# Windowed attention and a gated feed-forward layer on one core: a new order and new engines for every step, and the seven-product form from the fifth chunk on

## The chip, the core and the metric

One core of a Trainium2 chip runs the whole program. The metric is the device time of one execution in microseconds; less is better. The median of three runs of the kernel before is 890.99 us (888.37 to 891.76). The engines are TensorE (PE, with its weight loads as PEld), VectorE (DVE), ScalarE (ACT), GpSimd (POOL) and SyncE (SP), which here only issues DMAs.

## The reference

```
scores = q @ k^T / 8                        # 8 x 8 heads, 576 positions, 64 dims
scores = where(0 <= i - j < 64, scores, -1e9)
attn   = softmax(scores);  x = attn @ v     # x: 4608 tokens x 512
h   = x @ w_in                              # 512 -> 2048
g   = h * erf(softplus(h))
out = g @ w_out                             # 2048 -> 512
```

The inputs q, k and v are 32-bit floats, w_in and w_out 64-bit floats.

## The kernel before

All products on PE are made from 16-bit halves: each operand is scaled by a power of two and split into a high half and a low half, and three products (high by high, high by low, low by high) are summed. The other engines mostly make these halves.

**Weights.** Sixteen pieces of w_in and w_out are fetched by SP (L519), turned from 64-bit to 32-bit floats by DVE and ACT (L523, L527, L531), bounded (L537), and split: a high half (L346 on ACT, L348 on DVE, L350 on POOL) and a low half (L353 on DVE, or by PE at L580 and L581 and an eviction). PE fills the waits of this stage with warm-up products (L747).

**Attention**, in 36 tiles of 128 tokens. SP loads q, k and v; ACT or DVE take their largest magnitudes (L371, L373); a short chain of small DVE and PE steps (L380 to L398) makes the scales of a chunk of 256 tokens; q, k and v are split into halves (high: L346, L348 or L350; low: L353, always DVE). PE makes the scores (L425), DVE adds the mask and takes the maxima (L434), DVE or POOL subtracts them (L439), ACT takes the exponential (L443), and the result is split (L472, L474 or L476, and the remainder at L450 on DVE or POOL), turned by a DMA (L453) and multiplied with v (L460). DVE normalizes (L465 to L468); x is split (L472 or L474, L495) and turned by a DMA (L499).

**Feed-forward**, in 36 groups g: 18 chunks c of 256 tokens, each with the two halves of the 2048 hidden columns. The first matmul exists in two forms. The plain form (`mm1`, L620) has 4 pieces of 24 matmuls of 256 columns, and each piece is evicted once by ACT or DVE (`hidden`, L472 or L474). The seven-product form (`product`, L673) has 7 products of 24 matmuls of 128 columns; its inputs are sums of blocks of x (`x_sums`, L482) and of w_in (`w_sums`, L654 and L658, 72 steps in all, made once and kept in the three buffers named stage), and its outputs are 4 evictions (`take`, L472 or L474) and 3 additions on DVE (`add`, L689). Then come softplus and erf on ACT (L698, L702), the gate product on DVE (`gate`, L707), a high half (`g_hi`) and a low half (`g_lo`) of the gate, the second matmul with 16 + 8 matmuls of 512 columns in each half (`mm2`, L730), and the result on ACT or DVE (L346, L348, L739). ACT has to load another table when it goes from one of softplus, erf and exponential to another (ACT_TABLE_LOAD).

The constant `FAST` says from which chunk on the seven-product form is used; the chunks before it use the plain form. It also decides how the gate is split. In the plain chunks the high half is a scaling and the low half is always a SCALAR_TENSOR_TENSOR of DVE (L353); in the others the high half is a plain narrowing on ACT, DVE or POOL (L472, L474, L476), and the low half is a subtraction on DVE or POOL (L721):

```
def g_lo(g, n, eng="v"):
    if ORDER[g][0] < FAST:
        rest(glb[:, sl], yat(g, n), st_s[g][:, n:n + 1], ghb[:, sl])
    else:
        eng_of(eng).tensor_tensor(glb[:, sl], yat(g, n), ghb[:, sl], op=ALU.subtract)
```

**Order.** The string `PLAN` is the program: a list of steps such as `gl:14:0:g` (low half of the gate, group 14, half 0, on GpSimd; v is DVE, a is ACT) or `S:0:4:v` (step 4 of the sums of quarter 0 of w_in, on DVE). A loop at the end issues them one after the other, so the order of steps in the string is the order in every engine's queue and in the DMA queue of SP. Nothing is reordered later, and each engine works its queue in order. The short names that are used below: `mm` and `mw` are the pieces of the first matmul in its plain and its seven-product form, `mA` and `mB` the second matmul with the high and with the low half of the gate, `gh` and `gl` those halves, `xw` the additions at L689, `S` the sums of w_in, `xd` those of x, `dc` and `gn` small scale factors (L603, L609, L610), `h` the high halves of the weights, and `px` the small reduction at L388 and L389 inside the chain that makes a chunk's scales.

Of the kernel before, what the change touches and what calls it, by code (L numbers as in the profile page):

```python
# [18 lines left out]
B, H, S, D = 8, 8, 576, 64  # L19
W = 64  # L20
# [24 lines left out]
FAST = 5  # L45
# [770 lines left out]
```

## Time and profile before

| | |
|---|---|
| median of three runs | 890.99 us |
| the profiled execution, its own time | 889.82 us |
| its span, first to last instruction | 888.0 us |
| granted TensorE clock, mean | 0.988 |
| ACT table loads | 116 |
| matmuls in the first matmul, plain and seven-product | 960 and 4368 |

A row of a group gives the line, the engine, the operation, out<-in, shapes and count, then the busy time in us and the mean of one in ns, then the idle time of the engine just before them with what ended it. A row of the timeline gives the start and the length in us. A row by stage gives the start and end of the stage and its length, and then, for each engine, its busy time with the number of instructions in brackets.

### The profile page before, as it was taken

The page shows a single profiled execution, that of the slowest core. Times are in us where ns is not written, and L with a number is a line of the kernel's source. Part 1 is how long each engine was busy: PE and PEld are TensorE (multiplying, and loading weights), DVE is VectorE, ACT ScalarE, POOL GpSimd, SP SyncE. Part 2 cuts the span into 40 slices and gives each one's busy share as a digit, 9 for nine tenths or more (in the row PEclk, how much of TensorE's full clock was granted, in tenths as well). Part 3 has the DMA queues.
Part 4 walks back from the last instruction along what each step waited for, and adds up shares of the span by engine and source line. Part 5 has one row for each costly group of instructions (what it writes and reads, how often), then busy time and mean ns, then how long its engine had stood idle before and what let it go on. Part 6 is the DMA issues. An engine that isn't in the chain of part 4 may idle for free.

```text
span 888.0 us, 25679 instructions
## 1 busy us (share of the span) xinstructions
PE 845.5 (95%) x10915; PEld 594.2 (67%) x10915; DVE 760.8 (86%) x1623; ACT 656.9 (74%) x810; POOL 348.4 (39%) x276
## 2 busy tenths in 40 slices
PE   7879888999999999999899999999999999999998
PEld 4557566556666686766676776767776776777673
DVE  5999998999988999999888989897999898874642
ACT  6989987999796979787777876686656674673452
POOL 0315132621252246652336623075947262541201
PEclk9899999999999999999999999999999999999999
DMA  9985783343431646554536745445545452412000
GB/s 361 299 215 148 222 164 111 72 121 83 132 73 35 150 109 126 133 103 108 114 97 138 160 122 120 103 85 138 115 108 114 108 104 59 90 39 55 1 25 24
DMA packets 160515, 103.97 MB, mean 117 GB/s; under 512 B 137744, under 2 KB 137872, under 8 KB 160400
## 3 DMA queue, kind: packets, MB, share of 16 engines
q1 hardware_dynamic: 160400, 102.33, 47.0%
q8 instruction: 85, 1.39, 0.7%
q14 instruction: 30, 0.25, 0.1%
HBM read 59.44 MB, written 9.44 MB: 78 GB/s over the span
## 4 chain that ended last, share of the span: by engine, by line
PE 49%; DVE 25%; ACT 13%; DMA 5%; issue 5%; POOL 4%; SPq 0%; DVEq 0%; POOLq 0%; ACTq 0%
PE o L730 23%; PE hp L673 16%; PE hp L620 5%; ACT y L698 3%; DVE y L707 2%; DVE sm L434 2%; ACT L698 2%; DVE vs L353 2%; DVE h L689 2%; DVE p L450 2%; PE av L460 1%; ACT y L702 1%; PE s L425 1%; ACT L702 1%; DMA w<-w_in 1%
## 5 line engine op out<-in xcount | busy, mean ns | idle before, releaser
L730 PE MATMUL o<-w,gh 128*128 128x512 f16 x1152 | 260.7, 379 | 2.1 <-ACT gh L346 1.6
L730 PEld LDWEIGHTS <-gh 128*128 128x128 f16 x1152 | 109.7, 98 | 124.3 <-ACT gh L346 1.7
L673 PEld LDWEIGHTS <-w 128*128 128x128 f16 x2496 | 146.4, 98 | 22.8 <-issue 8.9
L673 PE MATMUL hp<-xt,w 128*128 128x128 f16 x2496 | 154.8, 220 | 6.4 <-DVE h L689 4.0
L730 PE MATMUL o<-w,gl 128*128 128x512 f16 x576 | 136.2, 379 | 0.0
L620 PE MATMUL hp<-xt,w 128*128 128x256 f16 x960 | 113.1, 277 | 6.7 <-ACT ks L346 3.7
L673 PE MATMUL hp<-xt,stage 128*128 128x128 f16 x1872 | 113.8, 219 | 4.1 <-DMA xt<-xs 2.4
L673 PEld LDWEIGHTS <-stage 128*128 128x128 f16 x1872 | 108.0, 98 | 13.1 <-issue 5.8
L721 POOL TENSOR_TENSOR gl<-y,gh 128x1024 f16<-128x1024 f32 x36 | 82.0, 2283 | 71.9 <-DVE gh L474 34.3
L620 PEld LDWEIGHTS <-w 128*128 128x128 f16 x960 | 94.0, 99 | 24.3 <-issue 7.7
L439 POOL TENSOR_TENSOR sm<-sm,mx 128x512 f32<-128x512 f32 x44 | 53.6, 1227 | 109.8 <-DVE mx L434 98.9
L698 ACT ACTIVATE y<-h,c 128x1024 f32<-128x1024 f32 x72 | 79.9, 1143 | 22.5 <-DVE h L474 22.1
L472 ACT ACTIVATE h<-hp 128x512 f32<-128x512 f32 x99 | 57.9, 587 | 51.6 <-PE hp L673 45.0
L730 PEld LDWEIGHTS <-gl 128*128 128x128 f16 x576 | 53.3, 98 | 54.3
L707 DVE SCALAR_TENSOR_TENSOR y<-h,cy,y 128x1024 f32<-128x1024 f32 x52 | 70.7, 1378 | 20.2 <-ACT y L702 19.8
L443 ACT ACTIVATE sm<-sm,shift,cde 128x512 f32<-128x512 f32 x72 | 57.4, 809 | 26.7 <-DVE sm L439 13.6
L702 ACT ACTIVATE y<-y 128x1024 f32<-128x1024 f32 x72 | 74.0, 1051 | 0.5
L689 DVE TENSOR_TENSOR h<-hp,h 128x512 f32<-128x512 f32 x78 | 53.1, 683 | 20.0 <-PE hp L673 13.1
L434 DVE CUSTOM_DVE_ANT_0 sm<-s,mask 128x128 f32<-128x128 f32 x288 | 65.1, 285 | 4.8 <-PE s L425 4.3
L698 ACT ACT_TABLE_LOAD x43 | 55.2, 1283 | 13.6 <-DVE h L474 8.5
L476 POOL TENSOR_SCALAR gh<-y 128x1024 f16<-128x1024 f32 x14 | 19.6, 1401 | 97.9 <-DVE y L707 97.9
L702 ACT ACT_TABLE_LOAD x44 | 56.5, 1283 | 0.8
(153 smaller groups left out, 1372.5 us busy)
## 6 DMA issues: line engine op xcount, KB each, us to landing
vr<-v_in SPq DMA_DIRECT2D x36, 512.0 KB, 4.3
kr<-k_in SPq DMA_DIRECT2D x36, 384.0 KB, 3.7
qr<-q_in SPq DMA_DIRECT2D x36, 256.0 KB, 3.4
out<-ob SPq DMA_DIRECT2D x36, 256.0 KB, 2.4
stage<-w_out SPq DMA_DIRECT2D x6, 1024.0 KB, 6.1
stage<-w_in SPq DMA_DIRECT2D x5, 1024.0 KB, 10.1
w<-w_in SPq DMA_DIRECT2D x2, 1024.0 KB, 11.5
w<-w_out SPq DMA_DIRECT2D x2, 1024.0 KB, 5.9
```

Of the source, the lines that this page charges most:

```text
L434: nc.vector.tensor_tensor_reduce(smi(u, par)[:, j, :], sps[par][:, j, :], mask[:, var, :], 1.0, LOWEST, op0=ALU.add, op1=ALU.max, accum_ou ...
L439: eng_of(eng).tensor_tensor(s, s, m.unsqueeze(2).broadcast_to([P, HP, P]), op=ALU.subtract)
L443: nc.scalar.activation(s, s, AF.Exp, bias=shift14, scale=es)
L472: nc.scalar.activation(dst, src, AF.Copy)
L620: nc.tensor.matmul(hps[pc % 2][:, f, :], w1[a][:, cc, fs], xt[b][c % 2][:, cc:cc + 5:4, :], start=(n == 0), stop=(n == 3 * NCC - 1))
L673: nc.tensor.matmul(dst, w, xt[b][c % 2][:, blk + cc, :], start=bool(first) and at + cc + a + b == 0, stop=at + cc + a == 3 * P + 2, skip_g ...
L689: nc.vector.tensor_tensor(dst, bank_of((1, 0, 1)[i]), dst, op=ALU.add)
L698: nc.scalar.activation(yat(g, n), at(hb, g, n), AF.Softplus, scale=st_c[g][:, n:n + 1])
L702: nc.scalar.activation(y, y, AF.Erf)
L707: nc.vector.scalar_tensor_tensor(y, at(hb, g, n), s, y, op0=ALU.mult, op1=ALU.mult)
L721: eng_of(eng).tensor_tensor(glb[:, sl], yat(g, n), ghb[:, sl], op=ALU.subtract)
L730: nc.tensor.matmul(ops[j], a[:, f, ts], w2[b][:, hf * GF + f, :], start=f == 0 and a is gh and b == 0, stop=f == GF - 1 and a is gl)
```

## The change

The whole of `PLAN` is written anew, and `FAST` goes from 5 to 4. No function is edited; since the string is one line longer, a line L of the kernel before is line L+1 in the changed kernel.

```
-FAST = 5
+FAST = 4
...
-    "gh:2:0:v mA:1:1 t:6:1 gl:1:1 er:2:1 gl:2:0 S:0:4:v sp:3:0 gt:2:1 a:6:0 sp:3:1 a:6:1 mB:1:1 pk:9:0:v gh:2:1:g "
...
+    "mA:35:0 gh:35:1:a mB:35:0 gl:35:1:v mA:35:1 mB:35:1 fo:35:0:v fo:35:1:v st:17:0 st:17:1 "
```

With `FAST` at 4, chunk 4 (groups 8 and 9) takes the seven-product form: 8 plain pieces go and 14 products come, with 6 additions, and the x of chunk 4 needs block sums. The sums of w_in must then be ready two groups earlier. Counted over the whole string, the steps move between engines as follows (before, after):

| step | ACT | DVE | POOL |
|---|---|---|---|
| low half of the gate (`gl`) | 0, 0 | 36, 50 | 36, 22 |
| high half of the gate (`gh`) | 43, 50 | 12, 11 | 17, 11 |
| sums of w_in (`S`) | 10, 8 | 35, 41 | 27, 23 |
| split of q, k, v, high half | 66, 73 | 28, 18 | 14, 17 |
| exponential, narrowing (`ec`) | 37, 28 | 18, 18 | 17, 26 |
| exponential, remainder (`r`) | 0, 0 | 40, 36 | 32, 36 |
| evictions of the first matmul (`ev`, `ew`) | 99, 97 | 45, 47 | 0, 0 |
| additions of the first matmul (`xw`) | 0, 0 | 78, 84 | 0, 0 |
| high half of the weights (`h`) | 10, 9 | 1, 5 | 5, 2 |
| largest magnitudes (`pk`) | 51, 57 | 57, 51 | 0, 0 |
| small scale factors (`dc`) | 0, 0 | 25, 15 | 11, 21 |

The built program holds 129 table loads on ACT, against 116, and 301 warm-up matmuls, against 293.

The first place is POOL's queue at groups 14 and 15. Before:

```order
L495 TENSOR_TENSOR xs_0_130<-x,xs_0_128 128x512
L721 TENSOR_TENSOR gl<-y_143,gh 128x1024
L721 TENSOR_TENSOR gl<-y_144,gh 128x1024
L439 TENSOR_TENSOR sm_118<-sm_118,mx_92 128x512
L450 TENSOR_TENSOR p_1_122<-sm_118,p_1_120 128x512
L482 TENSOR_TENSOR x<-x 128x256
L721 TENSOR_TENSOR gl<-y_142,gh 128x1024
L350 TENSOR_SCALAR ks_0_108<-kr_100,csc 128x768
L610 TENSOR_SCALAR sg<-kwo,cde,wm_67 128x1
L721 TENSOR_TENSOR gl<-y_143,gh 128x1024
```

And POOL's queue at groups 13 and 14 now, where gl is the low half of the gate, p and sm belong to the exponentials, and x is the attention's result:

```order
L722 TENSOR_TENSOR gl<-y_142,gh 128x1024
L477 TENSOR_SCALAR p_0_119<-sm_117 128x512
L451 TENSOR_TENSOR p_0_121<-sm_117,p_0_119 128x512
L722 TENSOR_TENSOR gl<-y_143,gh 128x1024
L477 TENSOR_SCALAR p_0_119<-sm_116 128x512
L440 TENSOR_TENSOR sm_118<-sm_118,mx_92 128x512
L451 TENSOR_TENSOR p_0_121<-sm_116,p_0_119 128x512
L483 TENSOR_TENSOR x<-x 128x512
L451 TENSOR_TENSOR p_1_122<-sm_118,p_1_120 128x512
L477 TENSOR_SCALAR p_1_120<-sm_116 128x512
```

Of the low halves of groups 14 and 15, all four of which were on POOL, one is left there (the second gl of the lower piece); narrowings and remainders of the exponentials stand where the others stood.

The second place is DVE's queue while the weights still arrive, at the tile 5 of the attention. Before:

```order
L353 SCALAR_TENSOR_TENSOR vs_1_115<-vr_103,csc,vs_1_113 128x16x64
L353 SCALAR_TENSOR_TENSOR vs_0_114<-vr_102,csc,vs_0_112 128x16x64
L353 SCALAR_TENSOR_TENSOR qs_1_107<-qr_99,csc,qs_1_105 128x512
L353 SCALAR_TENSOR_TENSOR ks_1_111<-kr_101,csc,ks_1_109 128x768
L531 SCALAR_TENSOR_TENSOR stage_149<-stage_149 128x1024
L450 TENSOR_TENSOR p_0_121<-sm_118,p_0_119 128x512
L439 TENSOR_TENSOR sm_116<-sm_116,mx_91 128x512
```

The same place of DVE's queue now; tmp is the running sum of blocks of w_in:

```order
L354 SCALAR_TENSOR_TENSOR vs_0_114<-vr_102,csc,vs_0_112 128x16x64
L354 SCALAR_TENSOR_TENSOR qs_1_107<-qr_99,csc,qs_1_105 128x512
L440 TENSOR_TENSOR sm_116<-sm_116,mx_91 128x512
L532 SCALAR_TENSOR_TENSOR stage_149<-stage_149 128x1024
L659 TENSOR_TENSOR tmp<-tmp,w_1_137 128x512
L451 TENSOR_TENSOR p_0_121<-sm_118,p_0_119 128x512
```

A step of the sums of w_in has come in between. DVE's first step of these sums is its row 214 now and was its row 256; ahead of the second matmul of group 4 it has eleven of them now and had six.

The third place is DVE's queue around the scales of the ninth chunk, at group 11. Before:

```order
L373 TENSOR_REDUCE peaks<-vr_103 128x1
L474 COPY h_140<-hp_155 128x2x2x128
L373 TENSOR_REDUCE peaks<-vr_102 128x1
L689 TENSOR_TENSOR h_140<-hp_154,h_140 128x2x2x128
L707 SCALAR_TENSOR_TENSOR y_144<-h_141,cy,y_144 128x1024
L380 TENSOR_REDUCE cmx<-peaks 128x3
L338 TENSOR_SCALAR cmx<-cmx 128x3
L439 TENSOR_TENSOR sm_116<-sm_116,mx_92 128x512
L450 TENSOR_TENSOR p_1_122<-sm_117,p_1_120 128x512
L388 TENSOR_REDUCE ctop<-av 3x1
L389 SCALAR_TENSOR_TENSOR cdiag<-ctop,ident 3x3
```

Now; cdiag is what PE waits for in the chain of scales:

```order
L349 TENSOR_SCALAR ob_147<-o_157,sg 128x512
L374 TENSOR_REDUCE peaks<-vr_103 128x1
L690 TENSOR_TENSOR h_140<-hp_155,h_140 128x2x2x128
L381 TENSOR_REDUCE cmx<-peaks 128x3
L339 TENSOR_SCALAR cmx<-cmx 128x3
L440 TENSOR_TENSOR sm_117<-sm_117,mx_93 128x512
L722 TENSOR_TENSOR gl<-y_144,gh 128x1024
L389 TENSOR_REDUCE ctop<-av 3x1
L390 SCALAR_TENSOR_TENSOR cdiag<-ctop,ident 3x3
```

The low half of the gate of group 11, second half, is now in DVE's own queue, ahead of the reduction; before it was in POOL's queue.

379 rows, old and new, of the table PLAN are left out of this document.

## The prediction, made before the changed kernel ran

> **What bounds the kernel now.** I read the head of the page first, then the busy times by stage, then the groups by line, then the timeline at the places where PE waits. About 0.5% (4.5 us) is what a measurement of this kernel can tell from no change.
>
> ```profile
> span 888.0 us, 25679 instructions
> PE 845.5 (95%) x10915; PEld 594.2 (67%) x10915; DVE 760.8 (86%) x1623; ACT 656.9 (74%) x810; POOL 348.4 (39%) x276
> ```
>
> PE is busy for all but 42.5 us of the span. The stages below are cut where the first piece of the first matmul starts (58.7) and where the second matmul of groups 1, 4, 9, 15, 20 and 34 starts.
>
> ```profile
> core 0: us, PE busy (x) PEld busy (x) DVE busy (x) ACT busy (x) POOL busy (x), PEclk, DMA share, GB/s
> 0.00:58.70 58.70, 44.02 (x542) 29.86 (x542) 47.24 (x116) 47.20 (x71) 12.83 (x28) 0.91 0.91 291
> 58.70:150.20 91.50, 81.57 (x1035) 61.79 (x1033) 84.67 (x211) 81.94 (x118) 26.05 (x25) 0.96 0.67 182
> 150.20:195.20 45.00, 44.91 (x387) 25.89 (x388) 43.24 (x81) 42.91 (x45) 20.80 (x16) 1.00 0.28 74
> 195.20:302.90 107.70, 105.83 (x1111) 70.33 (x1108) 98.73 (x214) 93.47 (x115) 31.80 (x28) 1.00 0.36 90
> 302.90:449.70 146.80, 139.90 (x2008) 102.65 (x2002) 137.28 (x297) 112.45 (x138) 70.53 (x52) 0.99 0.54 120
> 449.70:560.50 110.80, 108.74 (x1641) 78.39 (x1639) 99.43 (x233) 85.49 (x104) 45.83 (x34) 1.00 0.59 131
> 560.50:863.20 302.70, 299.54 (x4116) 216.02 (x4114) 242.92 (x472) 186.21 (x216) 137.40 (x91) 1.00 0.37 81
> 863.20:888.00 24.80, 21.03 (x99) 9.31 (x96) 7.28 (x7) 7.22 (x7) 3.17 (x2) 1.00 0.06 22
> ```
>
> What to see: from 58.7 to 150.2, PE idles 91.5 - 81.6 = 9.9 us while DVE is busy 93% of the stage and ACT 90%: weights and attention set the pace. From 150 to 303 PE idles only 2.0 us (0.09 + 1.87), but DVE has just 1.8 + 9.0 us free. From 303 to 450 PE idles 6.9 us again, with DVE at 94%; then 2.1 and 3.2 us, and 3.8 us at the end, where the last result is scaled and stored. So there are two limits: PE's own work, and DVE's queue where it is nearly full. A change gains by less PE work or by fewer of the waits that DVE hands to PE, and loses where it fills DVE before 303.
>
> **Term 1, PE's work in chunk 4.**
>
> ```profile
> L673 PE MATMUL hp<-xt,w 128*128 128x128 f16 x2496 | 154.8, 220 | 6.4 <-DVE h L689 4.0 <-DVE h L474 2.4
> L673 PE MATMUL hp<-xt,stage 128*128 128x128 f16 x1872 | 113.8, 219 | 4.1 <-DMA xt<-xs 2.4 <-DVE h L474 0.9 <-DVE h L689 0.5
> L620 PE MATMUL hp<-xt,w 128*128 128x256 f16 x960 | 113.1, 277 | 6.7 <-ACT ks L346 3.7 <-DMA xt<-xs 2.1 <-DVE h L474 0.6
> ```
>
> Matmuls overlap, so the busy time by the count is the cost: 113.1/960 = 0.118 us in the plain form, (154.8 + 113.8)/4368 = 0.0615 in the other. Out go 8 x 24 = 192 plain ones, 22.6 us; in come 14 x 24 = 336, 20.7 us. Term 1 is -2.0 us (rounded). Eight more warm-up matmuls sit in the first 60 us, where PE waits for weights anyway: nothing.
>
> **Term 2, the low halves that leave POOL.** The largest PE wait of the stage from 303 to 450 shows what such an instruction does:
>
> ```profile
> 415.47 4.40 POOL L721 TENSOR_TENSOR gl<-y,gh 128x1024 f16<-128x1024 f32 x2 [4.64 <-DVE gh L474]
> 415.54 2.35 DVE L474 CAST p<-sm 128x512 f16<-128x512 f32 x1 [0.23 <-ACT sm L443]
> 417.92 2.50 DVE L450 TENSOR_TENSOR p<-sm,p 128x512 f16<-128x512 f32 x1
> 421.67 0.68 DVE L450 TENSOR_TENSOR p<-sm,p 128x512 f16<-128x512 f32 x1
> 423.00 2.30 PE L673 MATMUL hp<-xt,w 128*128 128x128 f16 x28 [2.39 <-DVE h L474]
> 400.56 0.42 DVE L474 CAST p<-sm 128x512 f16<-128x512 f32 x1
> ```
>
> A DVE instruction that takes 0.42 or 0.68 us alone took 2.35 and 2.50 beside the two low halves on POOL: DVE was held until each ended, and 2.39 us of PE idle followed. The same pattern stands at two more PE waits of this stage:
>
> ```profile
> 355.91 2.22 POOL L721 TENSOR_TENSOR gl<-y,gh 128x1024 f16<-128x1024 f32 x1 [3.12 <-ACT gh L472]
> 356.37 1.77 DVE L389 SCALAR_TENSOR_TENSOR cdiag<-ctop,ident 3x3 bf16<-3x3 f32 x1
> 358.20 0.16 PE L392 MATMUL av<-cdiag,ones 128*128 128x3 bf16 x1 [0.83 <-DVE cdiag L389]
> 442.58 2.13 POOL L721 TENSOR_TENSOR gl<-y,gh 128x1024 f16<-128x1024 f32 x1
> 442.65 2.34 DVE L348 TENSOR_SCALAR qs<-qr,csc 128x512 f16<-128x512 f32 x1
> 445.64 1.50 PE L673 MATMUL hp<-xt,stage 128*128 128x128 f16 x24 [0.60 <-DVE h L474]
> ```
>
> Together 2.39 + 0.83 + 0.60 = 3.8 of the 6.9 us of PE idle. Of groups 10 to 15 ten low halves were on POOL, three are left; those behind all three waits have gone to DVE except one (group 14, first half).
>
> ```profile
> L721 POOL TENSOR_TENSOR gl<-y,gh 128x1024 f16<-128x1024 f32 x36 | 82.0, 2283 | 71.9 <-DVE gh L474 34.3 <-ACT gh L472 26.0 <-PE o L730 10.1
> L721 DVE TENSOR_TENSOR gl<-y,gh 128x1024 f16<-128x1024 f32 x16 | 21.6, 1350 | 0.6 <-POOL gh L476 0.3 <-PE o L730 0.2
> ```
>
> What DVE pays: each of the 14 that leave POOL is 1.35 us on DVE, and relieves DVE of a hold of 0 (a DVE instruction that needs nothing POOL holds) to 2.28 us. An instruction that arrives at random in a hold of 2.28 waits half, 1.1 us; I take 1 us. So DVE is at par over the whole run (14 x 0.35 = 5 us more), but the holds that hit a chain PE waits for are fewer. For PE I take -4 us: nearly all of the 3.8, and a little of the 2.1 after 450. Ends: 0, if the holds come back from POOL's other work, and -9, if all idle of both stages goes.
>
> **Term 3, DVE's debt before 303.** Ahead of the second matmul of group 9 the new order puts 9 additions, 8 sums of w_in, 4 sums of x, 3 evictions, 4 high halves of weights and 4 remainders more in DVE's queue, and 3 low halves of plain chunks less.
>
> ```profile
> L689 DVE TENSOR_TENSOR h<-hp,h 128x512 f32<-128x512 f32 x78 | 53.1, 683 | 20.0 <-PE hp L673 13.1 <-ACT h L472 5.4 <-PE av L392 1.0
> L658 DVE TENSOR_TENSOR tmp<-tmp,w 128x512 f32<-128x512 f32 x16 | 12.2, 765 | 1.9 <-POOL stage L654 1.3 <-POOL tmp L658 0.4
> L482 DVE TENSOR_TENSOR x<-x 128x256 f32<-128x256 f32 (+1 forms) x20 | 12.8, 638 | 1.5 <-POOL x L482 1.2
> L474 DVE COPY h<-hp 128x512 f32<-128x512 f32 x45 | 30.8, 685 | 14.1 <-PE hp L673 13.6 <-PE hp L620 0.3
> L348 DVE TENSOR_SCALAR w<-stage,sw 128x1024 f16<-128x1024 f32 x1 | 0.8, 753 | 0.0
> L450 DVE TENSOR_TENSOR p<-sm,p 128x512 f16<-128x512 f32 x40 | 37.1, 939 | 3.1 <-ACT p L472 2.2 <-POOL p L476 0.6
> L353 DVE SCALAR_TENSOR_TENSOR gl<-y,sy,gh 128x1024 f16<-128x1024 f32 x20 | 30.3, 1518 | 1.4 <-PE o L730 1.4
> ```
>
> 9 x 0.683 + 8 x 0.765 + 4 x 0.638 + 3 x 0.685 + 4 x 0.753 + 4 x 0.939 - 3 x 1.518 = 6.1 + 6.1 + 2.6 + 2.1 + 3.0 + 3.8 - 4.6 = 19 us; the rest (two low halves, larger halves of x, a gate more, fewer small scale factors) I estimate at +4 from rows of the same sizes. Neighbours on DVE overlap by about a tenth, so some 21 us of DVE time. Ahead of the same point PE has 8 plain pieces less and 19 products more: -22.6 + 456 x 0.0615 = +5.4 us, work done early, not added. So PE gets there 5.4 us later at no loss, and DVE's free time between 58.7 and 302.9 was 6.8 + 1.8 + 9.0 = 17.6 us. 17.6 + 5.4 = 23 against a need of 21: the queue just fits if DVE hardly idles. It does so from 150.2 to 195.2 (43.24 of 45.00, 96%). DVE's load is 84.7 + 43.2 + 98.7 = 226.6, plus 21 is 247.6; at 96% that takes 257.9 us where 249.6 are free, +8 us; at 99% 250.1, under +1. Idling as before, it is 21 - 5.4 = +16. I take +2, near the lower end, since a queue that is late stops waiting for others: most of DVE's idle time is such waiting. Queued behind a late DVE are the gate products, on which PE's second matmul waits. SP's queue has the transposes of x behind the same steps; chunk 4's are larger (1280 columns of x in place of 512), and PE has other pieces to do while they land: nothing.
>
> **ACT** has 13 table loads more.
>
> ```profile
> L702 ACT ACT_TABLE_LOAD x44 | 56.5, 1283 | 0.8
> L702 ACT ACTIVATE y<-y 128x1024 f32<-128x1024 f32 x72 | 74.0, 1051 | 0.5
> ```
>
> 13 x 1.283 = 16.7 us, against 231 us that ACT is free, most of it after 303. Where ACT is nearly full, from 58.7 to the second matmul of group 4, the order holds five of them: 6.4 us, against 9.6 + 2.1 = 11.7 us that ACT is free in those two stages (91.50 - 81.94 and 45.00 - 42.91). ACT's activations start with hardly any idle behind a load (0.5 us over 72). So it fits: nothing on the path; if that free time is gone to other work, up to 6.4 us, which is inside the bounds of term 3. [...]
>
> **The sum.** 888.0 - 2.0 - 4 + 2 = 884.0 span. The profiled execution's own time was 889.82, 1.8 above its span, which makes 885.8; the median of the runs is 1.2 above the profiled one, so 887.0.
>
> **The rivals.**
>
> *All of the idle goes.* No debt early, and the holds of both later stages go: 891.0 - 2.0 - 9.0 = 880. For it: each larger PE wait there but those on a DMA had a late DVE behind it. Against it: POOL still has 22 low halves, and three of the ten of groups 10 to 15.
>
> *DVE's queue becomes the bound before 303 (slower).* If DVE works below about 96% of the time between 58.7 and the second matmul of group 9, the debt is +8 to +16 and is never regained, since PE is full behind it: 891.0 - 2.0 - 4 + 12 = 897. For it: DVE idled 7% there with less to do. Against it: part of that idling was waiting for weights (DMA share 0.67 and 0.91 in the first stages), which new work can fill.
>
> *The holds change hands.* POOL has 9 narrowings, 4 remainders and 7 high halves of v more, and these hold DVE instead: 891.0 - 2.0 + 2 = 891, no change. For it: DVE's idle share hardly moves. Against it: these are shorter than 2.28 us.
>
> **Chances.** My forecast 0.42 (883 to 891), all idle goes 0.22, DVE the bound 0.25, holds change hands 0.11. Faster by over 0.5% means below 886.5: all of the first rival and half of the forecast, 0.43. Slower by over 0.5% means above 895.4: three quarters of the slower rival, 0.19. The rest, 0.38, is within. The forecast's own range is 883 to 891; the range from 878 to 898 leaves out the lower third of the first rival and the upper part of the slower one.
>
> **What would show it.** Right: the matmuls at the line of the seven products rise to 4704 and the plain ones fall to 768, PE's busy time falls by 2 us; PE's idle between the second matmuls of groups 9 and 15 falls from 6.9 to about 3 us, with no PE wait of over 1 us behind a low half on POOL; PE reaches the second matmul of group 9 at 308 to 312 us. Wrong: it gets there after 316 with DVE busy (the slower rival), before 306 (the first one), or the waits after 303 are as long as before, with other POOL instructions beside them (the third).

## The result, and the profile after

The changed kernel takes 884.16 us (median of six runs, 880.89 to 886.07), the kernel before on the same chip 890.8 (888.37 to 891.97): a ratio of 0.992, 95% interval 0.990 to 0.994, so 6.6 us less. The profiled execution is the shortest of the six, 880.89 us, so its span, 8.9 us below that of before, shows 2.3 us more than the medians do.

The head of the page after:

```profile
span 879.1 us, 25990 instructions
PE 838.2 (95%) x11067; PEld 592.7 (67%) x11067; DVE 735.5 (84%) x1617; ACT 675.6 (77%) x836; POOL 338.2 (38%) x280
```

PE's busy time fell by 7.3 us, its idle time only from 42.5 to 40.9. The stages, cut at the same steps as before:

```profile
0.00:57.90 57.90, 41.83 (x550) 29.28 (x550) 47.57 (x115) 44.25 (x68) 13.14 (x29) 0.94 0.86 292
57.90:146.50 88.60, 79.93 (x1034) 61.25 (x1034) 84.14 (x219) 85.53 (x122) 27.57 (x27) 0.98 0.65 190
146.50:198.80 52.30, 51.36 (x482) 31.21 (x483) 48.81 (x102) 50.38 (x55) 16.67 (x14) 1.00 0.35 90
198.80:304.20 105.40, 103.72 (x1276) 71.84 (x1275) 100.52 (x207) 89.94 (x113) 44.01 (x36) 1.00 0.41 97
304.20:445.30 141.10, 134.82 (x2056) 97.37 (x2049) 120.48 (x302) 112.54 (x142) 65.12 (x55) 0.99 0.56 124
445.30:548.50 103.20, 103.20 (x1450) 73.63 (x1447) 95.48 (x212) 82.35 (x101) 49.80 (x39) 1.00 0.57 126
548.50:851.90 303.40, 300.90 (x4116) 217.52 (x4113) 230.18 (x459) 203.43 (x234) 117.89 (x82) 1.00 0.35 80
851.90:879.10 27.20, 22.42 (x124) 10.59 (x121) 8.33 (x8) 7.22 (x7) 4.01 (x2) 1.00 0.07 28
```

Three things to see. DVE is at 85% between 304 and 445, where it was at 94%, and PE idles there nearly as long as before: 6.3 us against 6.9. From 58 to 146 the same number of matmuls, within one, takes 1.6 us less busy time, at a granted clock of 0.98 against 0.96. And the order puts other numbers of matmuls between the same milestones, so stages can't be compared by their lengths.

For that I use PE's *time beside its work*: when a step starts, less the pieces of PE ahead of it, each at the lower quartile of its spacing in the trace of before (a plain piece 2.62 us, a product 1.34, the second matmul 3.453 and 1.727). It holds idle time, slow clock and stalls together, whatever the order. For both kernels, and for experiments that follow:

| PE's time beside its work, us, up to | before | after | early_new | head_new | low_back | low_none |
|---|---|---|---|---|---|---|
| first piece of the first matmul | 39.2 | 38.4 | 38.0 | 39.0 | 38.5 | 38.5 |
| second matmul of group 1 | 56.0 | 52.3 | 52.5 | 57.6 | 57.1 | 55.9 |
| of group 9 | 60.8 | 57.7 | 57.9 | 62.2 | 63.2 | 62.0 |
| of group 15 | 72.5 | 68.5 | 66.7 | 71.1 | 76.0 | 72.2 |
| of group 20 | 76.2 | 69.6 | 70.3 | 74.7 | 77.9 | 75.2 |
| end | 87.4 | 80.7 | 81.4 | 85.9 | 97.5 | 94.7 |

Of the 8.9 us of span 2.2 are work that PE no longer has, 3.1 come off ahead of the second matmul of group 9, 0.9 up to group 15, 2.6 up to group 20, and 0.1 after that.

The early part by PE's waits (us in total, times, the longest), from the first piece of the first matmul to the second matmul of group 1. Before:

```profile
PE hp L620 <- ACT ks L346: 3.7, 1, 3.7
PE hp L620 <- DMA xt<-xs: 2.1, 2, 1.9
PE s L425 <- DVE ks L353: 0.9, 1, 0.9
```

After:

```profile
PE hp L621 <- DMA xt<-xs: 4.9, 3, 2.4
PE av L550 <- DVE wtop L547: 1.7, 1, 1.7
PE hp L621 <- ACT h L473: 1.5, 2, 0.9
```

The one wait of 3.7 us before a plain piece at 134.5 has become one of 2.4 at 131.5. The list of before puts it behind ACT's `ks`, which a plain piece doesn't read; in both traces it ends 0.13 to 0.14 us after a transpose of x has landed (at 134.36 before, 131.32 after), so it is a wait for x both times. The 1.6 us behind the high half of the gate, at the very end of that stage before, is gone too.

The late part, between the second matmuls of groups 9 and 20, after:

```profile
PE hp L674 <- ACT h L473: 3.0, 2, 2.1
PE o L731 <- ACT ob L347: 1.1, 1, 1.1
PE av L393 <- DVE cdiag L390: 1.0, 1, 1.0
```

The largest of these, in the timeline (start and length in us):

```profile
365.54 1.28 ACT L372 ACT_TABLE_LOAD   x1
366.72 2.40 POOL L483 TENSOR_TENSOR x<-x 128x512 f32<-128x512 f32 x2 [0.53 <-DVE x L469]
367.57 1.28 ACT L703 ACT_TABLE_LOAD   x1
368.86 1.06 ACT L703 ACTIVATE y<-y 128x1024 f32<-128x1024 f32 x1
369.83 0.58 ACT L473 ACTIVATE h<-hp 128x512 f32<-128x512 f32 x1
370.46 1.60 PE L674 MATMUL hp<-xt,stage 128*128 128x128 f16 x24 [2.05 <-ACT h L473]
```

PE waits for an eviction that stands in ACT's queue behind two table loads and an erf. The second load stands ahead of this erf in the kernel before too (at 365.22). The first is new: it is for a largest magnitude (`pk`, at 366.83) that was on DVE before and now stands on ACT between softplus and erf. Load and `pk` take the 2.03 us from 365.54 to 367.57, about the length of the wait. No low half on POOL is near. The wait of 2.39 us on DVE that the prediction showed, ahead of a product of group 15, is gone; this one of 2.05 us on ACT, ahead of a product of group 13, has come.

### The profile page after: what moved, and what is told of

The parts are those of the page before. It is cut to its first block, busy times and chain, and to the rows that moved or that the text cites. A ratio compares the mean times of both kernels' runs of the same rounds, so it can differ in the third digit from the quotient of the medians.

```text
span 879.1 us, 25990 instructions
## 1 busy us (share of the span) xinstructions
PE 838.2 (95%) x11067; PEld 592.7 (67%) x11067; DVE 735.5 (84%) x1617; ACT 675.6 (77%) x836; POOL 338.2 (38%) x280
## 4 chain that ended last, share of the span: by engine, by line
PE 50%; ACT 20%; DVE 15%; DMA 7%; issue 5%; POOL 2%; SPq 0%; POOLq 0%; ACTq 0%; DVEq 0%
PE o L731 25%; PE hp L674 21%; ACT y L699 4%; DMA kr<-k_in 3%; ACT L699 3%; ACT y L703 2%; ACT L703 2%; DVE y L708 2%; PE av L461 2%; ACT sm L444 2%; ACT h L473 2%; ACT L444 1%; DMA stage<-w_out 1%; PE s L426 1%; ACT junk L372 1%
## 5 line engine op out<-in xcount | busy, mean ns | idle before, releaser
L674 PEld LDWEIGHTS <-w 128*128 128x128 f16 x2688 | 157.1, 98 | 17.9 <-issue 3.9
L674 PE MATMUL hp<-xt,w 128*128 128x128 f16 x2688 | 165.6, 220 | 1.8 <-ACT h L473 1.3
L674 PE MATMUL hp<-xt,stage 128*128 128x128 f16 x2016 | 122.7, 219 | 4.3 <-ACT h L473 3.4
L674 PEld LDWEIGHTS <-stage 128*128 128x128 f16 x2016 | 116.3, 98 | 14.4 <-issue 5.4
L699 ACT ACTIVATE y<-h,c 128x1024 f32<-128x1024 f32 x72 | 80.0, 1143 | 27.0 <-DVE h L475 26.6
L440 POOL TENSOR_TENSOR sm<-sm,mx 128x512 f32<-128x512 f32 x44 | 65.6, 1494 | 89.0 <-DVE mx L435 81.8
L621 PE MATMUL hp<-xt,w 128*128 128x256 f16 x768 | 90.2, 276 | 7.3 <-DMA xt<-xs 4.9
L708 DVE SCALAR_TENSOR_TENSOR y<-h,cy,y 128x1024 f32<-128x1024 f32 x56 | 75.8, 1373 | 21.5 <-ACT y L703 21.4
L621 PEld LDWEIGHTS <-w 128*128 128x128 f16 x768 | 74.9, 99 | 22.9 <-issue 8.0
L722 POOL TENSOR_TENSOR gl<-y,gh 128x1024 f16<-128x1024 f32 x22 | 51.2, 2326 | 50.4 <-DVE gh L475 25.8
L690 DVE TENSOR_TENSOR h<-hp,h 128x512 f32<-128x512 f32 x84 | 57.4, 685 | 14.5 <-PE hp L674 12.4
L699 ACT ACT_TABLE_LOAD x45 | 57.7, 1283 | 9.2 <-DVE h L475 4.8
L451 POOL TENSOR_TENSOR p<-sm,p 128x512 f16<-128x512 f32 x36 | 47.9, 1335 | 35.7 <-DVE p L475 16.2
## 6 DMA issues: line engine op xcount, KB each, us to landing
w<-w_in SPq DMA_DIRECT2D x2, 1024.0 KB, 11.1
```

What stands on the lines that cost most here:

```text
L440: eng_of(eng).tensor_tensor(s, s, m.unsqueeze(2).broadcast_to([P, HP, P]), op=ALU.subtract)
L621: nc.tensor.matmul(hps[pc % 2][:, f, :], w1[a][:, cc, fs], xt[b][c % 2][:, cc:cc + 5:4, :], start=(n == 0), stop=(n == 3 * NCC - 1))
L674: nc.tensor.matmul(dst, w, xt[b][c % 2][:, blk + cc, :], start=bool(first) and at + cc + a + b == 0, stop=at + cc + a == 3 * P + 2, skip_g ...
L690: nc.vector.tensor_tensor(dst, bank_of((1, 0, 1)[i]), dst, op=ALU.add)
L699: nc.scalar.activation(yat(g, n), at(hb, g, n), AF.Softplus, scale=st_c[g][:, n:n + 1])
L708: nc.vector.scalar_tensor_tensor(y, at(hb, g, n), s, y, op0=ALU.mult, op1=ALU.mult)
```

## The experiments

Theory A: the gain is that of the low halves that left POOL, since each holds DVE. Theory B: order and engines were chosen for each other, and neither gains alone. Theory C: only PE's 2 us of work. All times are medians; ratios are to the kernel before on the same chip, with 95% intervals.

### Which half of the change, engines or order

**low_back**, the changed kernel with the low halves as before, 36 on POOL and not 22 (30 steps changed):

```diff
-gl:10:1:v ... gl:11:1:v ... gl:12:0:v ... gl:13:1:g
+gl:10:1:g ... gl:11:1:g ... gl:12:0:g ... gl:13:1:v
```

> The changed kernel with its order kept, but with the low halves of the gate on the engines that they had before: 36 of 72 on POOL again in place of 22. Theory A (the gain beside PE's work comes from fewer low halves on POOL, which hold DVE): the holds of DVE, 48 us in the changed kernel's trace against 85 before, come back by 14 x about 1 us, PE waits come back, and the time rises by 3 to 5 us over the changed kernel, to about 888 (ratio to before 0.996 to 0.998). Theory B (the order keeps DVE's work out of POOL's way, whoever does the low halves): the order was made for other engines, so some loss, 1 to 3 us, 885 to 887. Theory C (only PE's 2 us and chance): no change, 884 (0.992).

Measured: 896.24 us, 1.0069 (1.0047 to 1.0091): 12 us over the changed kernel. Behind the second matmul of group 9 its time beside the work is 34.3 us against 23.0. So in this order those 14 low halves are dear: 8.5 us of the difference arise behind the second matmul of group 20 (19.6 against 11.1), a part for which the prediction had no term.

**low_only**, the kernel before with the low halves of the changed kernel (28 steps, 20 on POOL):

```diff
-gl:10:1:g ... gl:11:1:g ... gl:12:0:g ... gl:13:1:v
+gl:10:1:v ... gl:11:1:v ... gl:12:0:v ... gl:13:1:g
```

> The kernel before with its order kept, and only the low halves of the gate on the engines that they have in the changed kernel: 20 on POOL in place of 36 (those of group 9 stay on DVE, which its plain form needs). Theory A: 16 holds of about 1 us go, DVE gains 16 x 1.35 us of work in their place, and PE loses some 3 to 4 us of waits: 887 (ratio 0.996). Theory B: moving them in an order that was made for POOL puts work into a DVE queue that is 94% full, so no gain or a loss: 890 to 895 (1.000 to 1.005). Theory C: 891.

Measured: 895.0 us, 1.0053 (1.0033 to 1.0074). The same move in the old order loses 5 us. Theory A, as a gain that goes with the low halves, falls here.

**fast5**, the changed order with chunk 4 in the plain form. Its plain pieces read blocks of w_in that the sums have replaced by then, so the work is the same but on other numbers:

```diff
-FAST = 4
+FAST = 5
-mw:8:2 mw:8:1 ew:8:0:a xw:8:0 ... xd:4:0 ...
+mm:8:0 ev:8:0:a ...
```

> The changed kernel's order and engines, with the seven-product form from the sixth chunk on as before: chunk 4's 14 products, 8 evictions and 6 additions become 8 plain pieces and 8 evictions at the same places, and its 3 sums of x go. PE gets back 2.0 us of work; DVE gives 6 x 0.68 + 3 x 0.64 = 6 us and some 3 us of larger halves of x back before 303. Theory A and B: PE is full there, so the time is 2 us over the changed kernel, 886 (0.994 to 0.995), less if the DVE work that goes was in PE's way. Theory C: all of the gain is the seven-product form, so the time goes back to 889 to 891 (0.998 to 1.000).

Measured: 891.47 us, 1.0006 (0.9988 to 1.0025). It loses 7.3 us, of which PE's work is 2.2. The plain pieces stand where products were planned, so this is no clean price of the form.

**letters_only**, the old order with all engines of the changed kernel (444 steps):

```diff
-h:4:a ... f:1:1:g ... ec:1:1:a ... dc:0:v
+h:4:v ... f:1:1:v ... ec:1:1:g ... dc:0:g
```

> The kernel before with its order kept, and every step on the engine that it has in the changed kernel (444 steps move between ACT, DVE and POOL); chunk 4 in the plain form. Theory A: the low halves are among the moves, so the holds fall by 15 us or more and the time by about 3 us, 888. Theory B: engines without the order that was made for them cost more than they give: each engine meets steps in an order that was timed for another's load, 895 to 905 (1.005 to 1.015). Theory C: 891.

Measured: 943.99 us, 1.0606 (1.0593 to 1.062).

**order_only**, the reverse: the changed order with the old engines (441 steps):

```diff
-h:4:v ... f:1:1:v ... ec:1:1:g ... dc:0:g
+h:4:a ... f:1:1:g ... ec:1:1:a ... dc:0:v
```

> The changed kernel's order with the engines of the kernel before (441 of the steps get another engine back; seven products from chunk 4 on, so steps that exist only in the new kernel keep theirs; 36 low halves on POOL). Theory B (order and engines were chosen for each other, neither is worth anything alone): well above the kernel before, at least as bad as low_back, where only 30 engines went back: over 900 us, as the engines without the order gave 944. Theory A (the low halves on POOL are what counts, the order is neutral): as low_back, about 896. Theory C (only PE's 2 us of work): 888 to 889.

Measured: 955.72 us, 1.0722 (1.0693 to 1.075). Theory B is borne out: either half of the change alone costs 53 to 64 us. C, which gave 891 and 888 to 889 for these two, falls with it.

### Which part of the program

**early_new**, the changed kernel up to the second matmul of group 9, the old order and engines behind:

```diff
 (changed kernel) ... ew:10:3:v e:12:0
-mA:9:0 m:13:0 f:13:0:v ...
+mA:9:0 (the kernel before, the steps not yet issued, in its order)
```

> The changed kernel as it is up to the second matmul of group 9, then the order and the engines of the kernel before for all that is left. By the difference of the two traces PE's idle and slow time falls by 3.1 us up to there and by 3.6 us behind it, and PE has 2.2 us less to do. Theory B (each part of the order carries its own gain): 890.8 - 2.2 - 3.1 = 885.5. Theory A (the gain is that of the low halves after that point, which stay on POOL here): 890.8 - 2.2 = 888.6. If the late part of the old order is only good behind the old early part, the seam costs and it is 890 or more.

Measured: 885.22 us, 0.9927 (0.9901 to 0.9954): the whole gain, within what can be told. Its head, its low halves, and its two stages from group 9 to 20:

```profile
PE 836.9 (95%) x11067; PEld 590.9 (67%) x11067; DVE 755.1 (86%) x1630; ACT 654.8 (74%) x809; POOL 354.2 (40%) x278
L722 POOL TENSOR_TENSOR gl<-y,gh 128x1024 f16<-128x1024 f32 x38 | 87.6, 2311 | 70.7 <-DVE gh L475 33.2
```

```profile
304.40:441.60 137.20, 131.05 (x1889) 94.26 (x1882) 125.03 (x283) 105.76 (x128) 66.12 (x48) 1.00 0.53 118
441.60:552.40 110.80, 108.75 (x1641) 78.36 (x1639) 99.43 (x233) 85.48 (x104) 46.17 (x34) 1.00 0.62 131
```

It has 38 low halves on POOL. By the trace, DVE's instructions beside them take about 34 us longer than their kinds do alone (each instruction's length less the lower quintile of its kind in the trace of before, counted to the POOL instruction that it overlaps most), against about 8 us in the changed kernel and 35 before. PE's largest waits between groups 9 and 20 are those of before too:

```profile
PE hp L674 <- DVE h L475: 3.7, 2, 2.4
```

Yet it is as fast as the changed kernel. The holds of the low halves are real, and PE waits behind some of them, but the gain doesn't hang on them. Theory A falls a second time.

**late_new**, the reverse: the kernel before up to that point, the changed order behind, chunk 4 plain:

```diff
 (kernel before) ... xt:11:1
-mA:9:0 (the kernel before)
+S:3:9:v S:3:10:v ... ew:10:3:v e:12:0 mA:9:0 (the changed kernel, the steps not yet issued, in its order)
```

> The kernel before as it is up to the second matmul of group 9, with the plain form in chunk 4, then the order and the engines of the changed kernel. Theory B and theory A both give the 3.6 us behind that point: 887.2. If the new late part is only good behind the new early part: 890 or more. Theory C (only PE's work): 890.8.

Measured: 899.92 us, 1.0091 (1.0064 to 1.0117), against 887 expected by A and B. The seam explains it: nine sums of w_in and the rest that the changed order has done by then now stand ahead of the matmul, and one wait ahead of it is long:

```profile
PE hp L673 <- ACT h L472: 7.2, 1, 7.2
```

Behind the seam its time beside the work is 24.9 us, against 26.6 before and 23.0 after. So this run says little of the late part, but gives no sign of a large gain there.

**head_old**, the changed kernel with the old order up to the second matmul of group 1:

```diff
-(changed kernel) ... h:14:a mA:1:0
+(kernel before) ... gh:1:1:a ... mA:1:0 (the changed kernel, the steps not yet issued)
```

> The changed kernel with the order and engines of the kernel before up to the second matmul of group 1 (seven products from chunk 4 on as in the changed kernel), then the changed kernel's. The traces show the early gain of 3.7 us (excess 56.0 against 52.3) in just that stretch, where weights land. If the order makes that gain: 884.2 + 3.7 = 888. If it is variation of the weight transfers from run to run: 884 to 885. If the sums of w_in, which the new order starts earlier, are late now: over 890.

Measured: 892.04 us, 1.0003 (0.9987 to 1.0019): undoing the first stretch alone loses 7.9 us, all of the gain. Part of that is a debt of sums of w_in at this seam too: 6.3 us beside the work between groups 1 and 4, where the changed kernel has 2.2.

**head_new**, the reverse, with no work of PE saved and no low half moved (36 on POOL). Theory D, formed on early_new, is that the first stretch makes the gain:

```diff
-(kernel before) ... gh:1:1:a mA:1:0
+(changed kernel) ... S:0:4:v ... S:0:7:v ... h:14:a gn:6:v ... gh:1:1:a mA:1:0 (the kernel before, the steps not yet issued)
```

> The changed kernel's order and engines up to the second matmul of group 1 (11 steps more stand ahead of it than before, 4 of them sums of w_in, and 4 fewer), then the kernel before in all that is left, with the plain form in chunk 4: no work of PE saved and no low half moved. Theory D (new after early_new: the gain beside PE's 2.2 us is made where the weights land, by a PE wait of 3.7 us behind ACT and one of 1.6 us in the old order, in whose place stands one of 2.4 us): in four runs with the old steps PE takes 16.8 to 18.9 us beside its work between the first piece of the first matmul and the second matmul of group 1, in four with the new ones 13.9, 14.4, 14.5 and 18.6; so 891 - 3 = 888. Theory A (the low halves): 891.

Measured: 886.65 us, 0.9942 (0.9923 to 0.9962): 3.4 to 6.9 us less than before, by the order and the engines of 519 steps that end at about 150 us (the four steps that the changed order has later still stand ahead of the matmul here). What is left to the changed kernel, 2.5 us by the medians, is about PE's saved work.

This profiled execution took 888.3 us, 1.65 over the median, and its own first stretch gained nothing (57.6 in the table above against 56.0). PE's waits in it from 58.5 to 151.9:

```profile
PE hp L620 <- DMA xt<-xs: 6.9, 4, 4.2
PE hp L620 <- ACT h L472: 2.0, 3, 1.1
```

So one execution can't show where the stretch gains; twelve can in part. Eight profiled executions have the new first stretch, order and engines, and four the old one. PE's time beside its work up to the second matmul of group 1 is 52.3 to 57.6 us in the eight, 54.8 in the mean, and 56.0 to 61.1 in the four, 58.5 in the mean: 3.7 us less (2.9 without head_old, which has eleven more steps there). The traces show three parts. The long wait for transposes of x was 2.4 to 2.8 us in five of the eight, 4.2 in three, and 3.6 to 4.2 in all four old ones. In those five the first of these transposes lands 0.5 to 0.6 us behind the last piece of w_out that is under way, in the three 2.1 us behind it; what decides between the two is not shown. The 1.6 us ahead of group 1 was there in all four old ones, and at most 1.0 us in the new. And from the first piece of the first matmul to group 1 the clock is halved for 6.4 us in the mean of the eight and 9.4 in the mean of the four, which is 1.5 us of time.

Behind group 9, where the steps of head_new are those of before, its trace gains 2.9 us of time beside the work. There 0.8 us net are PE idle: the wait of 2.39 us that the prediction showed is 1.10 here, with the same steps, since DVE's narrowing came 0.2 us ahead of the low half and wasn't held. And 1.7 us are the clock, halved for 3.4 us behind that wait in the trace of before and not in this one. Whether that is chance of one execution, or comes of the four sums of w_in that are out of the way by then, no run tells.

### What a low half on POOL costs in the changed order

Theory H: low_back paid for DVE held. Theory Q: for POOL's queue that comes late, and the later low half.

**low_twice** makes each of the 22 low halves twice, **narrow_twice** puts two narrowings ahead of each:

```diff
         if ORDER[g][0] < FAST:
             rest(glb[:, sl], yat(g, n), st_s[g][:, n:n + 1], ghb[:, sl])
         else:
+            if eng == "g":
+                nc.gpsimd.tensor_tensor(glb[:, sl], yat(g, n), ghb[:, sl], op=ALU.subtract)
             eng_of(eng).tensor_tensor(glb[:, sl], yat(g, n), ghb[:, sl], op=ALU.subtract)
```

```diff
         else:
+            if eng == "g":
+                narrow(eng, glb[:, sl], yat(g, n))
+                narrow(eng, glb[:, sl], ghb[:, sl])
             eng_of(eng).tensor_tensor(glb[:, sl], yat(g, n), ghb[:, sl], op=ALU.subtract)
```

> The changed kernel with each of the 22 low halves on POOL made twice, the second over the first with the same values: 22 x 2.33 = 51 us more on POOL, each low half ready 2.3 us later. Theory H (the cost in low_back is DVE held beside such an instruction): DVE held 8 us more or, at low_back's 0.58 each, 13 us more, and the time rises by 6 to 12 us, to 890 to 896. Theory Q (the cost in low_back is POOL's queue that comes late with other work, and the later low half): it rises as much as in narrow_twice.

> The changed kernel with two narrowings put ahead of each of the 22 low halves on POOL (of the gate, and of its high half, into the place of the low half, which is then written as before): about 22 x 2.2 = 48 us more on POOL, each low half ready 2.2 us later, but DVE is held little by a narrowing (0.1 us each in the changed kernel's trace). Theory H: about +1 to +3 us, 885 to 887. Theory Q: as much as low_twice.

Measured: 906.71 us, 1.0166 (1.0141 to 1.0192), and 904.48, 1.0142 (1.0113 to 1.0171); 22.5 and 20.3 us over the changed kernel. The heads of their pages, low_twice:

```profile
PE 845.8 (93%) x11067; PEld 594.1 (66%) x11067; DVE 762.8 (84%) x1617; ACT 676.6 (75%) x836; POOL 392.2 (43%) x302
```

narrow_twice:

```profile
PE 845.7 (94%) x11067; PEld 594.9 (66%) x11067; DVE 759.0 (84%) x1617; ACT 676.5 (75%) x836; POOL 397.7 (44%) x324
```

Equal times, as Q has it; but the premise of H failed, so the pair doesn't decide. With the same 1617 instructions DVE is busy 27.3 us longer in the one and 23.5 in the other: the added narrowings hold it nearly as much. What it does show is that 54 to 60 us (392.2 and 397.7 less 338.2) on an engine that is idle 62% of the time cost over 20 us.

**low_none** puts the 22 on DVE too:

```diff
-gl:11:0:g ... gl:14:0:g ... gl:16:1:g
+gl:11:0:v ... gl:14:0:v ... gl:16:1:v
```

> The changed kernel with the 22 low halves that POOL still has on DVE too: POOL loses 51 us, DVE gets 22 x 1.3 = 29 us and loses 8 us of holds. Theory A (fewer low halves on POOL is better): 881 to 884. Theory B (this order was made for just these engines): DVE's queue is late at places where PE waits for it, 888 or more.

Measured: 893.06 us, 1.0005 (0.9987 to 1.0023): 8.9 us over the changed kernel.

```profile
PE 839.3 (94%) x11067; PEld 591.7 (66%) x11067; DVE 755.3 (85%) x1639; ACT 675.7 (76%) x836; POOL 285.5 (32%) x258
PE hp L674 <- ACT h L473: 7.2, 8, 2.1
PE hp L674 <- DVE h L690: 6.9, 6, 2.2
```

More low halves on POOL and fewer both cost 9 to 12 us in the new order; 38 in the old late order cost nothing. There is no price of a low half on POOL that could be carried from one order to another.

## Why the prediction was right or wrong

The time was right: 887.0 predicted, 884.16 measured, faster by over 0.5%. Two of the three terms behind it were wrong, and their errors cancel, so the number was right by luck. Of the signs that the prediction named for being right, the counts of matmuls came, and no wait of over 1 us stands behind a low half; the others did not come. PE's arrival at 304.2 is the sign that it gave its first rival, and 6.3 us of idle come near that of its third; the time of neither (880 and 891) came.

**Term 1 held.** The rows after:

```profile
L674 PE MATMUL hp<-xt,w 128*128 128x128 f16 x2688 | 165.6, 220 | 1.8 <-ACT h L473 1.3
L674 PE MATMUL hp<-xt,stage 128*128 128x128 f16 x2016 | 122.7, 219 | 4.3 <-ACT h L473 3.4
L621 PE MATMUL hp<-xt,w 128*128 128x256 f16 x768 | 90.2, 276 | 7.3 <-DMA xt<-xs 4.9
```

22.9 us go and 19.7 come, 3.2 less by busy time; by the undisturbed spacing 8 x 2.62 - 14 x 1.34 = 2.2. head_new against the changed kernel leaves 2.5 us for it and all else. PE's busy time fell by 7.3 and not by 2; the row of the first stage holds 2.2 of that, where PE's warm-up products fill time, and 1.7 are the clock's: behind the first piece it is halved for 10.2 us in the trace of before (58.7, 133.8 and 424.0, 3.4 us each) and for 6.8 after (132.8 and 371.7).

**Term 2 failed**: "For PE I take -4 us: nearly all of the 3.8". The three waits behind low halves did go; but PE's idle in that stage went only from 6.9 to 6.3. The step that failed is taking the length of those waits for the gain, with nothing else late behind them. What is late there now is ACT, with 4.1 of the 6.3 us. The prediction costed ACT's 13 more table loads at nothing, behind 303 by ACT's free time as a whole; the wait at 370.46 stands behind one of them. The fall between groups 15 and 20 (idle 2.1 to 0.0) didn't come from the low halves either: early_new, with 38 of them on POOL, idles 2.1 there and ends as early. So the whole of the new late part, low halves and order together, is worth about 1 us (early_new less the changed kernel is +1.1 us, with overlapping intervals), and the term is about 0. The third rival, "The holds change hands", had PE's idle there right, but by other POOL instructions that hold DVE; the waits that came are mostly ACT's.

On table loads themselves the rows agree with the prediction's: 92 of the 129, and the activations behind 47 of them.

```profile
L699 ACT ACT_TABLE_LOAD x45 | 57.7, 1283 | 9.2 <-DVE h L475 4.8
L703 ACT ACT_TABLE_LOAD x47 | 60.3, 1283 | 0.8
L703 ACT ACTIVATE y<-y 128x1024 f32<-128x1024 f32 x72 | 73.6, 1052 | 0.5
```

A load took 1.283 us in both groups, and ACT idled 0.5 us in all ahead of the 72 activations.

**Term 3 failed in its sign**: "I take +2". The changed kernel reaches the second matmul of group 9 at 304.2 and not at 308 to 312, though PE had 4.4 us more work ahead of it (246.5 us there against 242.1). DVE's load between the first piece and that point rose from 226.6 to 84.1 + 48.8 + 100.5 = 233.5 us, by 6.9 and not 21. Some 8 of the missing 14 us are holds: DVE's instructions beside POOL's took about 17 us over their kinds' own time there before, about 9 after, and the prediction counted holds only behind 303. And the new order does more than shift steps: with its engines it makes the stretch where the weights land shorter. head_new measures that stretch at -4.8 us where +2 stood; the shorter waits and the clock shown there account for part of it, and the rest is open. The prediction treated the first 150 us as a queue that only gets fuller, and missed that the order could shorten the stretch of which it had said that "weights and attention set the pace".

**The sum.** With -2.2, 0 and -4.8 it is 7.0 us less, if the parts add; 6.6 were measured. The prediction had -2.0, -4 and +2.

**The slower rival** (DVE's queue the bound before 303) is not what happened here. order_only and letters_only don't show it either: about a third of their 53 to 64 us arises ahead of the second matmul of group 9, and their waits are spread over DVE, ACT and transfers.

## What to carry to other kernels

Where every engine's order is written out, engines and order are one choice: price neither alone. Here either half alone lost eight times or more of what both together gained. A wait that a profile shows behind a busy engine is worth its length only if nothing else is late just behind it; look along every queue that feeds the same step, ACT's table loads too. Compare several executions before a wait of one trace is given a price: the largest one here was 2.39 us in one execution and 1.10 in another with the same steps there. The first stretch, where data still arrives, is worth as much study as the stage with the most idle time: there nearly the same steps, in another order and on other engines, made most of the gain.

## What was not expected of the hardware

In places a PE wait of about 2 us cost twice here. The 10 us ahead of the wait of 2.39 us in the kernel before (420.6 to 423.0), the 10 us from its start on, and the 10 us after that (the third column from the right is the granted clock):

```profile
410.60:420.60 10.00, 10.00 (x188) 7.47 (x187) 9.31 (x8) 7.63 (x11) 4.63 (x3) 1.00 0.14 29
420.60:430.60 10.00, 7.61 (x65) 5.84 (x65) 9.15 (x30) 5.70 (x7) 3.63 (x3) 0.83 0.74 159
430.60:440.60 10.00, 10.00 (x85) 6.03 (x84) 7.50 (x12) 8.97 (x9) 1.46 (x1) 1.00 0.37 68
```

The 10 us behind the wait of 2.05 us in the changed kernel:

```profile
370.46:380.46 10.00, 10.00 (x105) 8.12 (x105) 8.56 (x17) 9.95 (x14) 2.63 (x2) 0.83 0.21 61
```

and about the end of one of 2.39 us in early_new (413.6 to 416.0), where the clock stayed whole:

```profile
415.90:425.90 10.00, 9.88 (x100) 6.74 (x100) 7.79 (x30) 7.78 (x9) 3.63 (x3) 1.00 0.48 132
```

0.83 over 10 us is 1.7 us lost: the traces' own records of the clock have it at half for 3.41 us there (424.0 to 427.4 before, 371.7 to 375.1 after). In the twelve profiled executions other than letters_only and order_only, between 200 and 860 us, 9 of the 20 waits of 1.7 us or more had a clock below 0.9 in the 10 us behind them (the shortest 1.75 us), and 2 of the 99 of 0.7 to 1.7.

The length of a wait alone doesn't tell the two kinds apart: 2.39 us had a halved clock behind it in the kernel before and a whole one in early_new, and in low_only a clock of 0.83 stood behind waits of 0.72 and 1.07 us.

In the records of the two kernels' own traces the changes of the clock lie 3.413 us or whole multiples of it apart; behind the start of the first matmul they are at 58.74, 62.15, 133.83, 137.24, 423.96 and 427.37 before, and at 132.78, 136.19, 371.71 and 375.12 after. Cut at these multiples, the slices just ahead of the five stretches of half clock hold 1.96, 3.07 and 2.39 us of PE idle before, 2.21 and 2.05 after. From there to 860 us no other slice holds more than 1.74 us (from 471.7, before), and none is followed by a half clock; in the first stage of before one with 1.72 us is (from 21.2). So in these two traces about 2 us of idle time in one slice were followed by 3.41 us at half the clock, 1.7 us of work. A sharp limit they don't show, and why early_new's wait of 2.39 us went without isn't shown either.

That may be a part of why executions of one program come to differ by 5 us (880.89 to 886.07); of these six, the one with the lowest mean clock (0.985) is not the longest, so it isn't all of it.
